# Second product: the high and low halves of B side by side, two matmuls in place of three

## The chip, the cores and the metric

One core of a Trainium2 chip runs the kernel. The metric is the device time of one execution in microseconds, as the median of several runs. The engines are TensorE (PE; its weight loads are listed as PEld), VectorE (DVE), ScalarE (ACT), GpSimd (POOL) and SyncE (SP), which issues most of the DMAs.

## The reference

Attention with a compressive memory for 4 batches x 8 heads x 576 positions x 64 dimensions, and behind it an expert layer over the 2304 rows that come out:

```
local = softmax(causal(q k^T / 8)) v
mem   = phi(q) M_prev / (phi(q) z_prev + 1e-6)        # phi(x) = elu(x) + 1
x     = (g * mem + (1 - g) * local) as [2304, 512]    # g = sigmoid(beta)
h     = x @ w_in                                      # [2304, 2048], the first product
r     = max(h, 0)
out   = (s * r * r + b) @ w_out                       # [2304, 512], the second product
```

## The kernel before

Precision comes from splitting. An fp32 operand x is kept as H = x rounded to fp32r and L = x - H, and a product of two such operands is H·H + H·L + L·H, three matmuls into one sum in PSUM.

The attention and the larger part of the first product are dealt out by a planner (class Plan). The rest of the first product is a hand-ordered list MM: L545 counts out what is left of batch 2, then for each of 16 column blocks f the 256 left-over rows (b = B, matmuls of 256 columns) and batch 3 (matmuls of 512 columns), each in two halves. t_mm1 issues one half, tick() moves a clock on by one, and later(n, ...) puts other work n ticks ahead. The outputs go through ScalarE's ReLU (L509) into r_d in DRAM.

Beside these ticks w_out is read as pairs of 32-bit words (load_u), converted (conv_u, conv64) and split. The second product is a Winograd form of a 2 x 2 block product: K is halved into KF = 8 blocks of 128, N into NE = 256 columns, rows into 128. It takes 7 products (numbered 1 to 7) for each of 9 tiles of 256 rows. split_u writes the high and low parts of five B operands into bHs and bLs, two tiles for each f. The B operands of products 4 and 2 (LATE) wait as fp32 in late32; late_b writes their high part into the room of w_in (slot w0H, free when half of the last ticks are done) and, in the first tile of the second product, their low part into w1H, which comes free with the last matmul of the first product.

For each tile, g_load reads r back into SRC, g_make squares, scales and shifts it (ScalarE), operand(t, m, c) makes the sums of A blocks and their H and L (two chunks c of four f each, eight buffers in all), product(t, m) issues 24 matmuls of 256 columns, and combine adds the results from PSUM into Y and U and stores them. SEQ is the order of the products; operands are issued AH = 2 products ahead, and g_make of the next tile from product 1 on. The source of even tiles lies in slot w0L, of odd tiles in w1L. The instructions of an engine run in order, and where the program does not pin it that order comes from the scheduler of the framework.

The lines that the change touches first of all are L714 to L716, the three matmuls, and L724 to L737, the additions.

Of the kernel before, what the change touches and what calls it, by code (L numbers as in the profile page):

```python
# [149 lines left out]
def attention_moe_kernel(  # L150
# [439 lines left out]
    PL = {m: n for n, m in enumerate((1, 3, 5, 6, 7))}  # L590
    w2 = ctx.enter_context(tc.tile_pool(name="w2", bufs=1, side="right", reuse_waits="tile"))
    bHs, bLs = {}, {}
    RAW = [0, 1, 2, 3, 4, 5, 6, 7, 4, 5, 6, 7, 8, 6, 7, 8]
    NRAW = 4
    NEXT = {n: (n + 4,) for n in range(9)} | {3: (), 4: (7, 8)} | {10: (13,), 11: (14,), 12: (15,)}

    def load_u(n):

        t = w2.tile([128, DM, 2], U32, tag=f"row{RAW[n]}", name="raw")
        r = n // 2 + n % 2 * KF  # L600
        nc.sync.dma_start(t, words(w_out)[128 * r:128 * r + 128])
        st["u", n] = t

    def stage(i):

        if i == 0:
            return stg0
        if i < 4:
            k = 4 + 2 * ((i + 1) % 2)
            return [w2.tile([128, 4, NE], F32, tag=f"bl{k + j}", name="stg1") for j in range(2)]  # L610
# [16 lines left out]
    def t_u(i, w, s):  # L627
# [6 lines left out]
        nc.vector.tensor_sub(late32[:, i, 0], t2, b21)  # L634

    def split_u(i, w, s):
        pin(nc.scalar.copy(late32[:, i, 1], w[:, 2]))
        bHs[i] = w2.tile([128, 5, NE], F32R, tag=f"row{i}", name="bH")
        bLs[i] = w2.tile([128, 5, NE], F32R, tag=f"bl{i}", name="bL")
        for x, a, n in ((w[:, 0:1], 0, 1), (w[:, 3:4], 1, 1), (s[:, 0:3], 2, 3)):  # L640
            L, H = bLs[i][:, a:a + n], bHs[i][:, a:a + n]
            pin(nc.scalar.copy(H, x))
            nc.vector.tensor_sub(L, x, H.bitcast(F32))

    def late_b(n, part):

        hs = slice(KF // 4 * n, KF // 4 * n + KF // 4)
        if part == 0:
            nc.scalar.copy(late[0][:, hs], late32[:, hs])
        else:  # L650
            nc.vector.tensor_sub(late[1][:, hs], late32[:, hs], late[0][:, hs].bitcast(F32))

    def b_op(m, f):
        if m in LATE:
            return [t[:, f, LATE.index(m)] for t in late]
        return bHs[f][:, PL[m]], bLs[f][:, PL[m]]

# [3 lines left out]
    def g_load(t):  # L661
        for f in range(0, NF, 4):
            c = 256 * (t % 2)
            nc.sync.dma_start(SRC[t % 2][:, f:f + 4], r_d[t // 2][:, f:f + 4, c:c + 256])
# [10 lines left out]
    def g_make(t, n):  # L675

        r = SRC[t % 2][:, NF // 4 * n:NF // 4 * n + NF // 4]
# [6 lines left out]
    def operand(t, m, c):  # L684

        r = SRC[t % 2]
        f1 = slice(4 * c, 4 * c + 4)
        f2 = slice(KF + 4 * c, KF + 4 * c + 4)
        A = {11: r[:, f1, 0:128], 12: r[:, f2, 0:128], 21: r[:, f1, 128:256], 22: r[:, f2, 128:256]}
        if m == 7 and not SUM:  # L690
# [5 lines left out]
        x = A[{1: 11, 7: 11, 5: 21, 6: 11, 3: 12, 2: 12, 4: 22}[m]]  # L696
# [11 lines left out]
    def product(t, m):  # L708
        ps = ps_y.tile([128, NE], F32, tag="y", name="yps")
        for f in range(KF):  # L710
            o = OPS[t, m, f // 4]
            H, L = o[:, 0, f % 4], o[:, 1, f % 4]
            BH, BL = b_op(m, f)
            nc.tensor.matmul(ps, lhsT=H, rhs=BH, start=f == 0, stop=False)  # L714
            nc.tensor.matmul(ps, lhsT=H, rhs=BL, start=False, stop=False)  # L715
            nc.tensor.matmul(ps, lhsT=L, rhs=BH, start=False, stop=f == KF - 1)  # L716
        OPS["ps", t, m] = ps

    def combine(t, m):
        ps = {n: OPS.get(("ps", t, n)) for n in SEQ}  # L720
        Y, U = YU[t % 2]
        add, sub = nc.vector.tensor_add, nc.vector.tensor_sub
        if m == 1:
            nc.scalar.copy(U[0], ps[1])  # L724
        elif m == 6:
            add(U[1], U[0], ps[6])
            add(U[2], U[1], ps[7])
            add(U[1], U[1], ps[5])
            add(Y[:, 1, NE:], U[2], ps[5])
            put_out(t, 1, slice(NE, DM), Y[:, 1, NE:])  # L730
        elif m == 3:
# [18 lines left out]
    stg0 = [w2.tile([128, 4, NE], F32, tag=f"row{i}", name="stg0") for i in (8, 7)]  # L750
    for i in range(4, 7):
        w2.tile([128, 5, NE], F32, tag=f"row{i}", name="row")
    late32 = w2.tile([128, KF, 2, NE], F32, tag="late", name="late32")
    for i in range(KF):
        w2.tile([128, 5, NE], F32, tag=f"bl{i}", name="blr")

    def slot16(tag, dtype):
        return wpool.tile([128, KF, 2, NE], dtype, tag=tag, name=tag)
# [94 lines left out]
```

## Time and profile before

| | us |
|---|---|
| median of 3 runs | 563.23 (560.71 to 563.55) |
| the profiled execution, its own time | 563.7 |
| its span | 561.6 |

Times in the profile's views are microseconds from the start of the span, unless marked ns. "Busy" of TensorE counts pipelined matmuls, so the length of one matmul is more than the distance to the next start. Where a view names what ended an engine's idle time, it stands in brackets with an arrow.

### The profile page before, as it was taken

What the parts mean: (1) busy time and instruction counts of PE and PEld (TensorE: products, weight loads), DVE (VectorE), ACT (ScalarE), POOL (GpSimd) and SP (SyncE); (2) the same over time, 40 slices, a digit from 0 to 9 for tenths busy, and PEclk for the clock granted to TensorE, in tenths of its full rate; (3) what the DMA queues carried; (4) which work ended last, traced back from release to release, by engine and by line L of the source; (5) the groups of instructions that cost most, each with busy time, mean ns of one, the idle gap of its engine ahead of it and who ended that gap; (6) DMA issues with size and microseconds to landing.
All of it is one profiled execution on the core that took longest, in us unless ns stands there. A gap on an engine that the chain in (4) does not pass through costs nothing.

```text
span 561.6 us, 11890 instructions
## 1 busy us (share of the span) xinstructions
PE 540.5 (96%) x4309; PEld 458.6 (82%) x4309; DVE 357.9 (64%) x884; ACT 399.4 (71%) x869; POOL 304.4 (54%) x327
## 2 busy tenths in 40 slices
PE   7978798999999999999999999999999999999997
PEld 5666576877777777777778888889999999999997
DVE  3888999999665264133309879137856786687562
ACT  5888977857867677246635657959779778877940
POOL 2587989577956646214310000324687678768850
PEclk9988999999999999999999999999999999999999
DMA  6643576684444441222147566447444435353101
GB/s 177 195 133 115 161 224 193 201 271 128 149 128 134 148 134 62 94 102 81 39 144 273 203 212 227 142 163 251 131 143 144 148 104 169 105 166 107 38 29 39
DMA packets 56666, 81.52 MB, mean 145 GB/s; under 512 B 7584, under 2 KB 39072, under 8 KB 56608
## 3 DMA queue, kind: packets, MB, share of 16 engines
q1 hardware_dynamic: 54592, 78.93, 44.2%
q10 hardware_dynamic: 2016, 1.84, 0.9%
q8 instruction: 34, 0.56, 0.4%
q14 instruction: 24, 0.20, 0.1%
HBM read 57.15 MB, written 23.59 MB: 144 GB/s over the span
## 4 chain that ended last, share of the span: by engine, by line
PE 87%; ACT 4%; DVE 4%; POOL 2%; issue 1%; POOLq 0%; ACTq 0%; DVEq 0%
PE yps L714 11%; PE yps L715 11%; PE yps L716 11%; PE sb L328 8%; PE tb L502 8%; PE tb L503 7%; PE tb L504 7%; PE sb L442 6%; PE hps L502 5%; PE hps L503 5%; PE hps L504 5%; PE tb L399 4%; ACT P L341 2%; DVE P L335 2%; POOL P L347 1%
## 5 line engine op out<-in xcount | busy, mean ns | idle before, releaser
L347 POOL TENSOR_SCALAR P<-P,sr,omg 128x192 f32<-128x192 f32 (+4 forms) x160 | 113.1, 724 | 58.0 <-DVE sr L375 37.4
L341 ACT ACTIVATE P<-P,mn 128x64 f32<-128x64 f32 (+4 forms) x160 | 88.6, 560 | 19.9 <-DVE mn L335 19.6
L714 PE MATMUL yps<-bH,op 128*128 128x256 f32 x360 | 101.2, 281 | 0.0
L715 PE MATMUL yps<-bL,op 128*128 128x256 f32 x360 | 101.1, 281 | 0.0
L716 PE MATMUL yps<-bH,op 128*128 128x256 f32 x360 | 101.1, 281 | 0.0
L335 DVE CUSTOM_DVE_ANT_0 P<-sb,mask 128x64 f32<-128x64 f32 (+4 forms) x160 | 69.8, 483 | 39.9 <-PE sb L328 39.8
L700 POOL TENSOR_TENSOR sum<-w0L 128x512 f32<-128x512 f32 x20 | 30.3, 1517 | 97.4 <-ACT w0L L680 75.8
L715 PEld LDWEIGHTS yps<-bL,op 128*128 128x128 f32 x360 | 67.9, 189 | 0.0
L716 PEld LDWEIGHTS yps<-bH,op 128*128 128x128 f32 x360 | 67.9, 189 | 0.0
L714 PEld LDWEIGHTS yps<-bH,op 128*128 128x128 f32 x360 | 67.8, 188 | 0.0
L328 PE MATMUL sb<-qk 64*128 64x288 f32 (+4 forms) x384 | 63.0, 450 | 2.7 <-DVE mn L335 2.7
L399 PEld LDWEIGHTS tb<-ident,P 64*128 64x128 f32 x928 | 40.3, 144 | 22.0 <-issue 5.5
L328 PEld LDWEIGHTS sb<-qk 64*128 64x128 f32 x384 | 41.1, 208 | 18.0 <-issue 8.0
L399 PE MATMUL tb<-ident,P 64*128 64x64 f32 x928 | 45.8, 234 | 10.0 <-POOL P L292 3.6
L523 ACT ACTIVATE r<-tb 128x512 f32<-128x512 f32 x41 | 24.4, 595 | 32.3 <-PE tb L504 26.4
L706 POOL TENSOR_TENSOR op<-w0L,op 128x512 fp32r<-128x512 f32 x30 | 42.4, 1433 | 6.3 <-ACT op L705 6.0
L409 ACT COPY pt<-tb 128x512 f32<-128x512 f32 x64 | 34.4, 589 | 11.0 <-PE tb L399 10.7
L700 POOL TENSOR_TENSOR sum<-w1L 128x512 f32<-128x512 f32 x16 | 24.5, 1531 | 31.9 <-DVE op L706 27.8
L705 ACT CAST op<-w0L 128x512 fp32r<-128x512 f32 x50 | 29.8, 615 | 16.1 <-PE yps L716 9.1
L502 PE MATMUL tb<-xs,w0H 128*128 128x512 f32 x96 | 40.4, 420 | 0.8 <-ACT pt L409 0.3
L714 PE MATMUL yps<-w0H,op 128*128 128x256 f32 x144 | 40.7, 283 | 0.0
L715 PE MATMUL yps<-w1H,op 128*128 128x256 f32 x144 | 40.7, 283 | 0.0
(136 smaller groups left out, 1439.7 us busy)
## 6 DMA issues: line engine op xcount, KB each, us to landing
r_d<-r SPq DMA_DIRECT2D x41, 256.0 KB, 2.1
w0L<-r_d SPq DMA_DIRECT2D x20, 512.0 KB, 4.7
qk<-in_qk_t_dram SPq DMA_DIRECT2D x15, 576.0 KB, 4.3
raw<-in_moe_w_out_dram SPq DMA_DIRECT2D x16, 512.0 KB, 5.3
w1L<-r_d SPq DMA_DIRECT2D x16, 512.0 KB, 4.5
xa<-in_moe_w_in_dram SPq DMA_DIRECT2D x12, 512.0 KB, 5.2
r_d<-r SPq DMA_DIRECT2D x48, 128.0 KB, 1.8
qs<-in_q_rows_dram SPq DMA_DIRECT2D x16, 320.0 KB, 4.0
```

Source lines behind the costliest of these rows:

```text
L328: nc.tensor.matmul(SB[ps[j]][:, o:o + n], lhsT=qk[rs, 128 * i:128 * i + 128], rhs=qk[rs, S + 64 + c0:S + 64 + c0 + n], start=True, stop=Tr ...
L335: nc.vector.tensor_tensor_reduce(P[:, j, PB[i] + 64:PB[i] + 64 + n], SB[ps[j]][:, o:o + n], m, -SCALE, 3.0e38, ALU.add, ALU.min, mn[:, j, ...
L341: nc.scalar.activation(pt, pt, AF.Exp, scale=-1.0, bias=mn[:, j, i:i + 1], accum_out=sm[:, j, i, 0:1])
L347: nc.gpsimd.tensor_scalar(pt, pt, sr[:, j, i:i + 1], omg[:, h:h + 1], ALU.mult, ALU.mult)
L399: nc.tensor.transpose(TB[ps[h]][:, o[h]:o[h] + 64], P[rs, j, c:c + 128], ident[rs, rs], tile_position=(64 * h, 0))
L502: nc.tensor.matmul(ps, lhsT=wH[:, p, fs], rhs=xs[:, 0], start=p == 0, stop=False)
L503: nc.tensor.matmul(ps, lhsT=wH[:, p, fs], rhs=xs[:, 1], start=False, stop=False)
L504: nc.tensor.matmul(ps, lhsT=wL[:, p, fs], rhs=xs[:, 0], start=False, stop=p == NP - 1)
L700: nc.gpsimd.tensor_sub(x, y, A[{7: 21, 3: 11}[m]])
L714: nc.tensor.matmul(ps, lhsT=H, rhs=BH, start=f == 0, stop=False)
L715: nc.tensor.matmul(ps, lhsT=H, rhs=BL, start=False, stop=False)
L716: nc.tensor.matmul(ps, lhsT=L, rhs=BH, start=False, stop=f == KF - 1)
```

## The change

B's high and low parts come to lie side by side in one tile (RB[i], shape [128, 5, 2, 256]; the late ones in two tiles of [128, 4, 2, 2, 256]). A step f of a product is then one matmul of H with 512 columns (BH and BL) and one of L with BH, 256 columns, onto the first half of the sum. The PSUM tile of a product is twice as wide, and combine adds both halves. SEQ is 1, 5, 6, 7, 3, 2, 4. The sign of late32's first part is turned, so product 4 is added. Both late parts are made as soon as the first slots w0H and w0L are free; the first tile's source takes the room of the fp32 late operands, the odd tiles' source takes w1H, and one of the output buffers w1L. The raw rows of w_out and their staging are dealt anew over the rooms of the B operands.

```diff
-    SEQ = [1, 7, 5, 6, 3, 2, 4]
+    SEQ = [1, 5, 6, 7, 3, 2, 4]
...
-        nc.vector.tensor_sub(late32[:, i, 0], t2, b21)
+        nc.vector.tensor_sub(T32[i // 2][:, i % 2, 0], b21, t2)
...
-        bHs[i] = w2.tile([128, 5, NE], F32R, tag=f"row{i}", name="bH")
-        bLs[i] = w2.tile([128, 5, NE], F32R, tag=f"bl{i}", name="bL")
+        RB[i] = w2.tile([128, 5, 2, NE], F32R, tag=f"rb{i}", name="rb")
...
-    def late_b(n, part):
-
-        hs = slice(KF // 4 * n, KF // 4 * n + KF // 4)
-        if part == 0:
-            nc.scalar.copy(late[0][:, hs], late32[:, hs])
-        else:
-            nc.vector.tensor_sub(late[1][:, hs], late32[:, hs], late[0][:, hs].bitcast(F32))
+    def late_b(n):
+
+        t = late[n // 2][:, 2 * (n % 2):2 * (n % 2) + 2]
+        H, L = t[:, :, :, 0], t[:, :, :, 1]
+        nc.scalar.copy(H, T32[n])
+        nc.vector.tensor_sub(L, T32[n], H.bitcast(F32))
...
-        if m in (7, 3):
-            y = x
-            x = SUM[c]
-            nc.gpsimd.tensor_sub(x, y, A[{7: 21, 3: 11}[m]])
-        elif m == 5:
-            nc.vector.tensor_add(x, x, A[22])
+        x = {1: a11, 5: SUM[c], 6: SUM[c], 2: a12, 7: a21, 3: SUM[c], 4: a22}[m]
+        if m == 5:
+            nc.vector.tensor_add(x, a21, a22)
         elif m == 6:
-            nc.vector.tensor_sub(x, A[21], x)
+            nc.vector.tensor_sub(x, x, a11)
+        elif m == 7:
+            nc.gpsimd.tensor_sub(x, a11, x)
+        elif m == 3:
+            nc.gpsimd.tensor_sub(x, a12, x)
...
-        ps = ps_y.tile([128, NE], F32, tag="y", name="yps")
+        ps = OPS["ps"] = ps_y.tile([128, 2, NE], F32, tag="y", name="yps")
         for f in range(KF):
             o = OPS[t, m, f // 4]
             H, L = o[:, 0, f % 4], o[:, 1, f % 4]
-            BH, BL = b_op(m, f)
-            nc.tensor.matmul(ps, lhsT=H, rhs=BH, start=f == 0, stop=False)
-            nc.tensor.matmul(ps, lhsT=H, rhs=BL, start=False, stop=False)
-            nc.tensor.matmul(ps, lhsT=L, rhs=BH, start=False, stop=f == KF - 1)
+            B = b_op(m, f)
+            nc.tensor.matmul(ps, lhsT=H, rhs=B, start=f == 0, stop=False)
+            nc.tensor.matmul(ps[:, 0], lhsT=L, rhs=B[:, 0], start=False, stop=f == KF - 1)
...
+        def onto(y, x):
+            add(y, x, ps[:, 0])
+            add(y, y, ps[:, 1])
+
+        if m in (1, 5):
+            u = U[0 if m == 1 else 3]
+            nc.scalar.copy(u, ps[:, 1])
+            add(u, u, ps[:, 0])
         elif m == 6:
-            add(U[1], U[0], ps[6])
-            add(U[2], U[1], ps[7])
-            add(U[1], U[1], ps[5])
-            add(Y[:, 1, NE:], U[2], ps[5])
+            onto(U[1], U[0])
+        elif m == 7:
+            onto(U[2], U[1])
+            add(U[1], U[1], U[3])
+            add(Y[:, 1, NE:], U[2], U[3])
             put_out(t, 1, slice(NE, DM), Y[:, 1, NE:])
         elif m == 3:
-            add(Y[:, 0, NE:], U[1], ps[3])
+            onto(Y[:, 0, NE:], U[1])
...
-            later(0, g_load, 0)
+            late.extend(slot16(f"w0{n}", F32R, [4, 2, 2, NE]) for n in "HL")
             for i in range(4):
-                later(LT + i, g_make, 0, i)
+                later(max(i, begin + CT[4 * i + 3] + 5 - clock[0]), late_b, i)
+            later(LT, first_load)
             for i in range(4):
-                later(max(LT + 4 + i, begin + CT[4 * i + 3] + 5 - clock[0]), late_b, i, 0)
+                later(LT + 6 + 2 * i, g_make, 0, i)
             for i in range(4):
-                later(LT + 8 + i, operand, 0, SEQ[i // 2], i % 2)
+                later(LT + 15 + i, operand, 0, SEQ[i // 2], i % 2)
...
-            if t == 0 and i < 4:
-                late_b(i, 1)
```

## Rows read from the trace of the kernel before

**Rows 1.** The page: busy us, share of the span, instructions of each engine.
```profile
PE 540.5 (96%) x4309; PEld 458.6 (82%) x4309; DVE 357.9 (64%) x884; ACT 399.4 (71%) x869; POOL 304.4 (54%) x327
```

**Rows 2.** Windows: length, busy PE, PEld, DVE, ACT, POOL, clock, DMA, GB/s.
```profile
292.00:378.00 86.00, 86.00 (x469) 74.85 (x470) 55.79 (x112) 58.04 (x126) 8.47 (x6) 1.00 0.62 207
378.00:558.00 180.00, 179.64 (x1513) 179.44 (x1511) 119.52 (x169) 136.50 (x198) 121.67 (x84) 1.00 0.39 124
438.00:458.00 20.00, 20.00 (x171) 20.00 (x170) 14.48 (x21) 16.16 (x24) 15.21 (x11) 1.00 0.44 134
```

**Rows 3.** By source line: count, duration ns min/median/max, first and last start.
```profile
L714 PE MATMUL yps<-bH,op x360: 277/281/285, 378.0 to 551.4; 128*128 128x256 f32 x180
...
L716 PE MATMUL yps<-w0H,op x144: 278/283/283, 392.4 to 557.4; 128*128 128x256 f32 x144
```

**Rows 4.** Timeline of TensorE, end of the first product: start, length, instruction.
```profile
365.42 0.28 PE L502 MATMUL hps<-x,w1H 128*128 128x256 f32 x1
365.53 0.28 PE L503 MATMUL hps<-x,w1H 128*128 128x256 f32 x1
...
366.85 0.40 PE L502 MATMUL hps<-xs,w1H 128*128 128x512 f32 x1
367.08 0.40 PE L503 MATMUL hps<-xs,w1H 128*128 128x512 f32 x1
367.32 0.39 PE L504 MATMUL hps<-xs,w1L 128*128 128x512 f32 x1
...
369.60 0.28 PE L502 MATMUL hps<-x,w1H 128*128 128x256 f32 x1
```

**Rows 5.** Groups, 378 to 558: busy, mean ns, idle before.
```profile
L706 DVE TENSOR_TENSOR op<-sum,op 128x512 fp32r<-128x512 f32 x34 | 23.3, 718 | 0.6 <-ACT op L705 0.6
...
L704 DVE TENSOR_TENSOR w0L<-w0L 128x512 f32<-128x512 f32 x8 | 13.2, 1653 | 0.9 <-POOL op L706 0.9
...
L702 DVE TENSOR_TENSOR w0L<-w0L 128x512 f32<-128x512 f32 x8 | 8.9, 1108 | 4.3 <-ACT w0L L680 4.3
...
L726 DVE TENSOR_TENSOR yu<-yu,yps 128x256 f32<-128x256 f32 x9 | 3.8, 421 | 42.0 <-PE yps L716 42.0
...
L724 ACT COPY yu<-yps 128x256 f32<-128x256 f32 x9 | 3.2, 352 | 0.7 <-PE yps L716 0.7
```

**Rows 6.** Timeline of the end, TensorE's last matmul and VectorE's last addition.
```profile
557.36 0.28 PE L716 MATMUL yps<-w0H,op 128*128 128x256 f32 x1
557.68 0.42 DVE L737 TENSOR_TENSOR yu<-yu,yps 128x256 f32<-128x256 f32 x1 [2.45 <-PE yps L716]
```

**Rows 7.** Waits from 378 to 558 (us, times, longest), then timeline in one tile.
```profile
ACT op L705 <- PE yps L716: 14.5, 19, 1.3
...
449.37 0.42 DVE L726 TENSOR_TENSOR yu<-yu,yps 128x256 f32<-128x256 f32 x1 [4.05 <-PE yps L716]
449.82 0.42 DVE L727 TENSOR_TENSOR yu<-yu,yps 128x256 f32<-128x256 f32 x1
...
452.71 3.46 POOL L706 TENSOR_TENSOR op<-w0L,op 128x512 fp32r<-128x512 f32 x2
```

**Rows 8.** Late operand and first tile: timeline, then the group of one line.
```profile
346.82 2.07 SPq L664 DMA_DIRECT2D w0L<-r_d  x4
...
353.03 1.04 ACT L649 CAST w0H<-late 128x1024 fp32r<-128x1024 f32 x1
...
349.46 1.29 DVE L643 TENSOR_TENSOR bL<-stg,bH 128x256 fp32r<-128x256 f32 x2
362.17 0.69 DVE L702 TENSOR_TENSOR w0L<-w0L 128x512 f32<-128x512 f32 x1 [11.42 <-issue]
...
362.94 3.00 POOL L706 TENSOR_TENSOR op<-w0L,op 128x512 fp32r<-128x512 f32 x2 [1.92 <-ACT op L705]
...
L651 DVE TENSOR_TENSOR w1H<-late,w0H x4: 1218/1220/1221, 379.9 to 383.3; 128x1024 fp32r<-128x1024 f32 x4
```

More of the change, by code (lines that the diff above doesn't have):

```diff
@@ L590, in attention_moe_kernel, with room @@
     PL = {m: n for n, m in enumerate((1, 3, 5, 6, 7))}
+    STG = {0: 7, 1: 6, 2: 5, 3: 7}
+    NEXT = {n: (n + 4,) for n in range(6)} | {7: (10, 11)} | {n: (n + 4,) for n in range(8, 12)}
     w2 = ctx.enter_context(tc.tile_pool(name="w2", bufs=1, side="right", reuse_waits="tile"))
[L592 to L595, printed above, removed]
+    RB = {}
+    T32 = [w2.tile([128, 2, 2, NE], F32, tag=f"late{i}", name="late32") for i in range(KF // 2)]
+    def room(k, dtype, name):
+        t = w2.tile([128, 2, 1280], dtype, tag=f"rb{k}", name=name)
+        return [t[:, h, :1024] for h in range(2)]
     def load_u(n):
-        t = w2.tile([128, DM, 2], U32, tag=f"row{RAW[n]}", name="raw")
+        if n % 2 == 0:
+            st["raw"] = room(n // 2, U32, "raw")
+        t = st["raw"][n % 2].rearrange("p (c b) -> p c b", b=2)
         r = n // 2 + n % 2 * KF
@@ L604, in stage @@
     def stage(i):
[L606 to L610, printed above, removed]
+        if i in STG:
+            return [t.rearrange("p (a e) -> p a e", e=NE) for t in room(STG[i], F32, "stg")]
         return stg[2 * (i % 2)], stg[2 * (i % 2) + 1]
@@ L661, in g_load @@
     def g_load(t):
-        for f in range(0, NF, 4):
+        for n in range(4):
             c = 256 * (t % 2)
-            nc.sync.dma_start(SRC[t % 2][:, f:f + 4], r_d[t // 2][:, f:f + 4, c:c + 256])
+            nc.sync.dma_start(SRC[t % 2][n], r_d[t // 2][:, 4 * n:4 * n + 4, c:c + 256])
     def put_out(t, h, cs, y):
@@ L675, in g_make @@
     def g_make(t, n):
[L677 removed]
+        r = SRC[t % 2][n]
         order = pin if t else same
@@ L686, in operand @@
         r = SRC[t % 2]
[L687 to L690, printed above, removed]
+        a11, a12, a21, a22 = r[c][:, :, 0:128], r[2 + c][:, :, 0:128], r[c][:, :, 128:256], r[2 + c][:, :, 128:256]
+        if not SUM:
             both = w2.tile([128, 2, 4, 128], F32, tag="row8", name="sum")
@@ L746, in attention_moe_kernel, with first_load, slot16 @@
     SUM = []
-    LT = 2
-    for i in range(NRAW):
-        load_u(i)
[L750 to L758, printed above, removed]
+    LT = 5
+    def first_load():
+        SRC.append([w2.tile([128, 4, 256], F32, tag=f"late{i}", name="src0") for i in range(4)])
+        g_load(0)
+    for i in range(4):
+        load_u(i)
+    for i in range(2, KF):
+        w2.tile([128, 2, 1280], F32, tag=f"rb{i}", name="rb")
+    def slot16(tag, dtype, shape):
+        return wpool.tile([128, *shape], dtype, tag=tag, name=tag)
     begin = clock[0]
@@ L778, in attention_moe_kernel @@
     flush()
-    late.append(slot16("w1H", F32R))
-    SRC.append(slot16("w1L", F32).rearrange("p f a (b n) -> p (f a b) n", n=256))
+    both = slot16("w1H", F32, [4, 4, 256])
+    SRC.append([both[:, n] for n in range(4)])
     YU = []
-    for t in (x4pool.tile([128, 2048], F32, tag="x4", name="yu0"), w2.tile([128, 2048], F32, tag="late", name="yu1")):
+    for t in (x4pool.tile([128, 2048], F32, tag="x4", name="yu0"), wpool.tile([128, 2048], F32, tag="w1L", name="yu1")):
         YU.append((t[:, :1024].rearrange("p (j e) -> p j e", j=2),
-                   [t[:, 1024 + NE * k:1024 + NE * k + NE] for k in range(3)]))
+                   [t[:, 1024 + NE * k:1024 + NE * k + NE] for k in range(4)]))
     p3.close()
```

27 lines of the change are left out of this document (10 added, 17 removed).

## The prediction

> **What bounds the kernel now.** I read the page first, for the busy shares: TensorE is busy for 96% of the span, no other engine for more than 71% [rows 1]. An average over stages says little about one stage, so next come the windows by stage. The change touches two of them. From 292 to 378 us (the end of the first product) TensorE is busy for all of 86.00 us, and from 378 to 558 (the second product) for 179.64 of 180.00, at a granted clock of 1.00, the level of 2.4 GHz, in both [rows 2]. Nothing stalls TensorE in the second product, so what it costs is the spacing of its matmuls. The by-line view gives that spacing: the first matmul starts at 378.0, the last at 557.4, and there are 9 tiles x 7 products x 8 x 3 = 1512 of them, so (557.4 - 378.0) / 1511 = 0.1187 us each [rows 3]. The listed 0.28 us of one matmul is its pipelined length and no part of a sum. The other engines follow from the window of one tile of 20 us: VectorE 14.48 busy, ScalarE 16.16, GpSimd 15.21 [rows 2]. They are beside the path, but not by much, and this decides how much of a gain can be kept.
>
> **Matmuls: three become two.** For each of 8 x 63 = 504 steps, H x BH and H x BL (256 columns each) become one matmul of 512 columns, and L x BH stays. The columns are the same 768; what goes is one matmul with its weight load. Before, a step costs 3 x 0.1187 = 0.3562 us. The kernel already runs matmuls of 512 and 256 columns next to each other at the end of the first product [rows 4], and two prices come out of that stretch. (a) At the seams: 512 after 256 takes 367.08 - 366.85 = 0.23, 256 after 512 takes 365.53 - 365.42 = 0.11, a step of 0.34. (b) A whole round of twelve 256s and twelve 512s: 369.60 - 365.42 = 4.18, divided by 12 is 0.348. In the new order every matmul stands at a seam, so (a) is the nearest row, but it is a difference of two times printed to 0.01 (0.32 to 0.36 with rounding), while (b) is averaged. I take 0.346, between them and nearer to the averaged one. That saves 0.3562 - 0.346 = 0.0102 us a step, 504 x 0.0102 = 5.1 us. The bounds: 0.348 saves 4.1 us; 0.34 saves 8.2 us.
>
> The rows thus show a fixed part in every matmul: two 256s cost 2 x 0.1187 = 0.237 us, one 512 some 0.227 to 0.229 (0.346 or 0.348 less 0.1187), so 8 to 10 ns go with the instruction and not with its columns. The Trainium skill (TensorE: Matmul & The Clock Gate, section "Wait — 56ns, not 53.3ns?") puts the fixed part of a warm matmul at about 2.5 ns. By that page the change would save 504 x 2.5 ns = 1.3 us, an estimate from the page alone. The trace does not agree, with 8 to 10 ns [rows 3, 4].
>
> **Combining: one sum in PSUM becomes two.** H x BL now collects in columns of its own, so each product needs one addition more. Per tile VectorE goes from 7 additions that read PSUM to 14, at 0.42 us each [rows 5]: 2.9 us more of VectorE, and one copy of 0.35 us more of ScalarE. They lie beside the matmuls, except the last one: after the final matmul starts at 557.36, the addition at 557.68 and the output DMA are the path to the end [rows 6]. The second of two dependent additions starts 0.45 us after the first (449.37 and 449.82, where one uses the other's result) [rows 7]. The tail grows by 0.45 us.
>
> Beside the matmuls the cover is as follows. A tile's 168 matmuls at 0.1187 are 19.94 us now, and its 56 steps at 0.346 will be 19.38. VectorE then needs 14.48 + 2.9 = 17.4 of 19.38 us, ScalarE 16.2 + 0.4 = 16.5, GpSimd its same 15.2. So all fit, VectorE with 2.0 us to spare where it had 5.5. What can spoil that is order. VectorE runs in order, and today it waits for TensorE at almost one place in a tile alone: the first addition of product 6, 42.0 us for 9 of them, 4.7 us a tile [rows 5]. After the change every product ends with additions, seven such places, and those of products 1 and 5 wait for a ScalarE copy too. Behind a waiting addition stand the sums and low parts of the next operands, and TensorE waits for these. Against that stands the lead: ScalarE waits 19 times for TensorE to free an operand buffer [rows 7], so operands are as far ahead as the eight buffers let them, and GpSimd starts on the low parts of a tile's first operand at 452.71 [rows 7], while that product starts only at about 458 (product 6 ends at 449.4 by the addition it releases, and three more of 2.85 us follow). The work takes 3.46 us, which leaves about 2 us of slack. The PSUM pool has eight buffers, one for each product, so a late addition alone stops nothing. I cost this edit at nothing, and its bound is in the rivals.
>
> SEQ changes too (1, 5, 6, 7 for 1, 7, 5, 6), with the same number of sums per tile; product 5 is now second, so its sum a21 + a22 is due one product earlier. These sums are the slow ones: 1.65 and 1.11 us on average, for a size that the low part of a sum takes 0.72 for [rows 5]. No fewer of them are made, so I see no gain here; the cost is zero or the stall of rival 1.
>
> **The late operands and the first tile's source.** Before, the high part of the late operand is made in the first product and its low part in the second, four subtractions of 1.22 us at 379.9 to 383.3 [rows 8]. These move up into VectorE's empty time between 350.8 and 362.2 [rows 8]: nothing, and 4.9 us less for VectorE in the first tile. But their room pushes the first tile's source out: it now takes the place of late32, so the load has to wait for the late operand, where before it was issued at 346.82 [rows 8]. From that load to the end of GpSimd's low parts of product 1's operand (362.94 + 3.00 = 365.9) it was 19.1 us, ReLUs of the stores, squares, scales and casts included. The last quarter of the new load can be issued when ScalarE's last late copy (353.03 + 1.04) and its subtraction (1.22) are done, at 355.3, so the operand is there at 355.3 + 19.1 = 374.4. It is due at 378.0 [rows 3], product 5's operand 2.8 us later. That leaves 3.6 us. On SyncE the stores of r stand behind the waiting load; held up for some us, they hold ScalarE's ReLUs, and these the pool of eight PSUM tiles, each of which takes TensorE 2.1 us on average (4.18 us for two, [rows 4]), so 16 us of cover. I cost it at nothing; the bound is 2.8 us, if the 19.1 us become a third more.
>
> The raw weights, stage buffers and their places are re-dealt, with the same 16 loads, conversions and splits. Their end at 350.8 [rows 8] starts the chain above, and a shift by 3 us stays within its slack. The first four loads may wait a little longer or shorter for room; nothing but this chain hangs on them.
>
> **The sum.** The profiled execution took 563.7 us by its own time (span 561.6, 2.1 around it). 563.7 - 5.1 + 0.45 = 559.05. It lies 0.5 us above the median of 563.23, so against the median I say 558.6.
>
> **The rivals.**
> 1. Operand stalls eat half of the gain or all of it. With 2.0 us of VectorE to spare a tile, TensorE would stop for 0.3 to 0.6 us a tile, where a sum for product 5 or 6 meets GpSimd's work behind a waiting addition: 9 x 0.3 to 0.6 = 2.7 to 5.4 us, so 561.3 to 564.0. For it: 17.4 of 19.38 us. Against: the lead, and no stall today. 18%.
> 2. VectorE becomes the bound, the case on the other side. Its place is the seven ordered waits of a tile, its price the part of them that exceeds 2.0 us. Today's waits are 4.7 us a tile in one place. If 3.2 us of them stay, a tile takes 17.4 + 3.2 = 20.6, 1.2 us over 19.38, and 9 tiles give 11 us: 569.6; with 3.8 it is 575. It is slower than before from 2.5 us of waits a tile on (0.5 over, times 9, is the whole gain). Against: a wait shrinks when its engine runs late. 10%.
> 3. The start of the second product is missed: the chain above lands past 378 by 2 to 3 us, 560.6 to 561.6. 6%.
> 4. The fixed part goes with the columns and not with the instruction, so the change doesn't do what it says: a 512 costs 2 x 0.1187 = 0.237 and the step 0.356, no gain, and the tail on top gives 563.7. The slowest 512 comes near (367.08 to 367.32 is 0.24 [rows 4]). 5%. The Trainium skill's page, with its 2.5 ns, would come close to this time: 563.7 - 1.3 + 0.45 = 562.9, or 562.4 against the median.
> 5. Steps at 0.34: 555.5. 8%.
>
> **Chances.** The forecast has 53%. A measurement of this kernel can tell about 0.5%, so 560.4 is the border. Faster, the forecast and rival 5 with the mildest end of rival 3: 0.62. Same, rivals 1, 3 and 4 for the most part: 0.26. Slower, rival 2 and a bad end of rival 1: 0.12. The range from 555.5 to 563.8 leaves out rival 2, the worst of rival 1 and a little below, some 16%.
>
> **What would show it.** In the profile after, the steady step should be 0.340 to 0.349 with the 512s near 0.23 and 256s near 0.11; the second product should last 504 x 0.346 = 174.4 us in place of 179.6, with no gap longer than a step. The window of a tile should have VectorE near 17.4, and the first product should still be full from 292 on and end at 378.0. Gaps before the first matmul of a product, above all of 5 and 6, released by VectorE, would be rivals 1 and 2; a gap at 378 rival 3; a 512 at 0.237 rival 4. The prediction is wrong in its core if the step is outside 0.340 to 0.349 or if TensorE is less than 99% busy after 378.

## The result

The changed kernel takes 567.86 us (median of 4 runs, 567.84 to 570.09) against 562.88 for the kernel before on the same chip: a ratio of 1.0105, 95% interval 1.0068 to 1.0142. It is about 1% slower, where 558.6 us, and so faster, was forecast. The profiled execution of after took 567.84 us by its own time (span 565.7), 4.1 us more than the one of before (563.7).

The page of after, engines (busy us, share, instructions), and the first line of its chain, beside [rows 1]:

```profile
PE 539.5 (95%) x3805; PEld 431.8 (76%) x3805; DVE 407.4 (72%) x947; ACT 400.0 (71%) x878; POOL 305.6 (54%) x327
...
PE 61%; DVE 16%; ACT 14%; issue 4%; POOL 4%; ACTq 0%; POOLq 0%; DVEq 0%
```

504 matmuls are gone (4309 to 3805), TensorE's share falls, and 30% of the chain runs through VectorE and ScalarE, where the page of before has 8%. The windows of after, columns as in [rows 2]:

```profile
292.00:378.00 86.00, 86.00 (x472) 74.93 (x471) 61.84 (x118) 59.26 (x130) 7.40 (x6) 1.00 0.59 206
...
400.00:550.00 150.00, 145.44 (x812) 123.61 (x812) 134.99 (x188) 117.64 (x174) 103.87 (x72) 1.00 0.35 111
...
438.00:458.00 20.00, 19.44 (x110) 16.47 (x109) 17.63 (x28) 16.33 (x24) 14.07 (x11) 1.00 0.43 131
```

The first product is as full as before. In the second, TensorE is idle for 4.56 us of 150, where it was idle for 0.36 of 180 [rows 2]. In the window of 20 us VectorE and ScalarE sit where the prediction put them, at 17.6 and 16.3. The granted clock is 1.00 as before.

From its first matmul to its last the second product takes 376.55 to 560.96 = 184.41 us, 5.0 more than before (179.4, [rows 3]). Its nine tiles, from the first matmul of one to that of the next (the ninth: to its own last), take 19.52, 19.70, 20.51, 20.73, 20.27, 20.91, 20.79, 20.98 and 21.0 us; before, each took 19.95. So the first two tiles gain and the others lose.

**Who keeps TensorE waiting.** The waits of after from 376 to 562 (us, times, longest):

```profile
ACT op L704 <- DVE sum L699: 26.6, 14, 3.4
...
PEld yps L714 <- DVE op L705: 9.2, 15, 1.5
```

TensorE waits for low parts (L705), and ScalarE, which casts the high parts (L704), waits for VectorE's sum for product 6 (L699). The wait that [rows 7] showed before, ScalarE for `PE yps` (19 times, a buffer not yet free), is down to two in this window. ScalarE's timeline shows why (start, length, instruction, idle before and releaser; it is busy without a gap in the lines left out):

```profile
441.14 1.23 ACT L704 CAST op<-sum 128x512 fp32r<-128x512 f32 x2 [3.41 <-DVE sum L699]
...
455.33 1.24 ACT L681 ACTIVATE src<-src,b_sb,s_sb 128x1024 f32<-128x1024 f32 x1
456.48 0.60 ACT L704 CAST op<-sum 128x512 fp32r<-128x512 f32 x1
457.60 0.62 ACT L704 CAST op<-sum 128x512 fp32r<-128x512 f32 x1 [0.52 <-DVE sum L697]
461.62 0.62 ACT L704 CAST op<-sum 128x512 fp32r<-128x512 f32 x1 [3.41 <-DVE sum L699]
```

VectorE and GpSimd at the same place:

```profile
454.95 0.84 DVE L697 TENSOR_TENSOR sum<-src,src 128x512 f32<-128x512 f32 x1 [1.34 <-ACT src L681]
...
456.60 0.91 DVE L697 TENSOR_TENSOR sum<-src,src 128x512 f32<-128x512 f32 x1 [0.48 <-ACT src L681]
...
457.76 3.15 DVE L705 TENSOR_TENSOR op<-sum,op 128x512 fp32r<-128x512 f32 x2
460.83 0.68 DVE L699 TENSOR_TENSOR sum<-sum,src 128x512 f32<-128x512 f32 x1
```
```profile
456.91 3.46 POOL L701 TENSOR_TENSOR src<-src 128x512 f32<-128x512 f32 x2
```

This is a loop that closes over one tile. VectorE's sum for product 5 (L697) waits for ScalarE's last shift of the tile's source (L681). ScalarE's next casts wait for that sum and for the one of product 6 (L699), which on VectorE stands behind the low parts of product 5. And behind these casts, in ScalarE's order, stand the squares and shifts of the next tile (L680, L681), for which the next sums will wait. TensorE is not part of it. One turn, from one cast to the same a tile later, takes 461.62 - 441.14 = 20.48 us: ScalarE's work of the tile and 3.9 us of waits at the seam. The four turns from 441.14 on, up to 524.30, take 20.8 us on average.

**It was there before.** ScalarE's casts of product 6 in the trace of before, and in the last line a cast that waits for a free buffer:

```profile
440.35 0.62 ACT L705 CAST op<-w1L 128x512 fp32r<-128x512 f32 x1 [2.29 <-DVE w1L L704]
...
456.81 0.62 ACT L705 CAST op<-w0L 128x512 fp32r<-128x512 f32 x1 [0.99 <-DVE w0L L704]
459.71 0.62 ACT L705 CAST op<-w0L 128x512 fp32r<-128x512 f32 x1 [2.28 <-DVE w0L L704]
...
495.01 0.62 ACT L705 CAST op<-w0L 128x512 fp32r<-128x512 f32 x1 [0.86 <-PE yps L716]
```

One turn took 459.71 - 440.35 = 19.36 us, and TensorE's tile 19.95, so the loop hid with 0.59 us to spare. The turns around it are as long: the same cast starts at 421.00, 440.35, 459.71, 479.06 and 498.43. The new loop, in the turn shown, is 1.1 us longer (0.35 of it the second copy, 0.7 longer waits, 3.93 for 3.27), against a TensorE tile that is only 0.27 us shorter (19.68, in e5 and e7 below).

### The profile page after: what moved, and what is told of

Read it like the earlier page. It is cut to its first block, busy times and chain, and to the rows that moved or that the text cites. A ratio compares the mean times of both kernels' runs of the same rounds, so it can differ in the third digit from the quotient of the medians.

```text
span 565.7 us, 10940 instructions
## 1 busy us (share of the span) xinstructions
PE 539.5 (95%) x3805; PEld 431.8 (76%) x3805; DVE 407.4 (72%) x947; ACT 400.0 (71%) x878; POOL 305.6 (54%) x327
## 4 chain that ended last, share of the span: by engine, by line
PE 61%; DVE 16%; ACT 14%; issue 4%; POOL 4%; ACTq 0%; POOLq 0%; DVEq 0%
PE sb L328 8%; PE tb L502 8%; PE tb L503 6%; PE tb L504 6%; PE sb L442 6%; DVE op L705 6%; PE hps L502 5%; PE hps L503 5%; PE hps L504 5%; PE tb L399 4%; PE yps L713 4%; ACT op L704 4%; POOL P L347 2%; DVE sum L697 2%; PE yps L714 2%
## 5 line engine op out<-in xcount | busy, mean ns | idle before, releaser
L713 PE MATMUL yps<-rb,op 128*128 128x512 f32 x360 | 126.6, 394 | 0.0
L714 PE MATMUL yps<-rb,op 128*128 128x256 f32 x360 | 101.8, 285 | 4.6 <-DVE op L705 4.4
L705 POOL TENSOR_TENSOR op<-src,op 128x512 fp32r<-128x512 f32 x30 | 41.8, 1412 | 90.1 <-ACT op L704 86.2
L713 PEld LDWEIGHTS yps<-rb,op 128*128 128x128 f32 x360 | 67.3, 188 | 14.8
L714 PEld LDWEIGHTS yps<-rb,op 128*128 128x128 f32 x360 | 67.8, 188 | 9.4 <-DVE op L705 9.2
L704 ACT CAST op<-sum 128x512 fp32r<-128x512 f32 x54 | 33.4, 620 | 38.6 <-DVE sum L699 26.6
L705 DVE TENSOR_TENSOR op<-sum,op 128x512 fp32r<-128x512 f32 x54 | 53.9, 1014 | 8.0 <-ACT op L704 7.9
L502 PE MATMUL tb<-xs,w0H 128*128 128x512 f32 x96 | 40.3, 420 | 0.8 <-ACT pt L409 0.3
L292 POOL TENSOR_TENSOR P<-qs,nrm 128x384 f32<-128x384 f32 (+1 forms) x30 | 23.5, 802 | 31.0 <-PE tb L399 15.4
L705 POOL TENSOR_TENSOR op<-w1H,op 128x512 fp32r<-128x512 f32 x24 | 32.9, 1395 | 12.3 <-PE yps L714 5.5
L503 PE MATMUL tb<-xs,w0H 128*128 128x512 f32 x96 | 37.7, 392 | 0.0
L504 PE MATMUL tb<-xs,w0L 128*128 128x512 f32 x96 | 37.5, 390 | 0.0
L509 ACT ACTIVATE r<-hps 128x256 f32<-128x256 f32 x62 | 21.3, 384 | 16.2 <-DMA r_d<-r 11.8
```

The costliest lines, as they stand in the source:

```text
L502: nc.tensor.matmul(ps, lhsT=wH[:, p, fs], rhs=xs[:, 0], start=p == 0, stop=False)
L503: nc.tensor.matmul(ps, lhsT=wH[:, p, fs], rhs=xs[:, 1], start=False, stop=False)
L504: nc.tensor.matmul(ps, lhsT=wL[:, p, fs], rhs=xs[:, 0], start=False, stop=p == NP - 1)
L705: (nc.gpsimd if m in ONPOOL else nc.vector).tensor_sub(L, x, H.bitcast(F32))
L713: nc.tensor.matmul(ps, lhsT=H, rhs=B, start=f == 0, stop=False)
L714: nc.tensor.matmul(ps[:, 0], lhsT=L, rhs=B[:, 0], start=False, stop=f == KF - 1)
```

## The experiments

Four theories stand in the expectations. A, in its first form, puts the loop down to the room that the sums of products 5 and 6 share; A2 is the loop through ScalarE's order as above. B: VectorE has too much to do (seven more additions a tile). P: the new places of the operands, or the late operands, cost the time. "Steady tile" is the distance between first matmuls of neighbouring tiles, for the sixth to the eighth tile of the profiled execution; the second product runs from its first matmul's start to its last one's. In e1, e2 and so on the edit is to the kernel after unless another is named.

| | median us | ratio to before, 95% interval | second product us | steady tile us |
|---|---|---|---|---|
| after | 567.86 | 1.0105, 1.0068 to 1.0142 | 184.4 | 20.8 to 21.0 |
| e1 own room for sum 6 | 566.76 | 1.0059, 1.0039 to 1.0080 | 184.1 | 20.5 to 20.6 |
| e2 old order | 566.35 | 1.0053, 1.0031 to 1.0075 | 182.4 | 20.83 |
| e3 no second additions | 568.04 | 1.0086, 1.0057 to 1.0116 | 184.8 | 20.9 to 21.1 |
| e4 three matmuls | 568.27 | 1.0085, 1.0059 to 1.0111 | 185.4 | 21.05 |
| e5 no shift pass | 560.70 | 0.9949, 0.9932 to 0.9966 | 176.9 | 19.68 |
| e6 old order, three matmuls | 562.11 | 0.9984, 0.9967 to 1.0002 | 179.4 | 19.95 |
| e7 old order, no second additions | 559.62 | 0.9938, 0.9909 to 0.9966 | 176.9 | 19.68 |
| e8 e1 without second additions | 567.22 | 1.0073, 1.0045 to 1.0101 | 183.8 | 20.5 to 20.7 |
| e9 before, casts doubled | 570.28 | 1.0138, 1.0100 to 1.0176 | 187.8 | 20.9 to 21.4 |
| e10 shift folded | 582.30 | 1.0329, 1.0293 to 1.0366 | 189.5 | 21.2 to 22.4 |
| e11 old order, folded | 567.69 | 1.0081, 1.0054 to 1.0108 | 176.3 | 19.53 |
| e12 e11, root moved | 569.41 | 1.0107, 1.0073 to 1.0141 | 176.3 | 19.53 to 19.56 |
| e13 e11, root held late | 559.98 | 0.9968, 0.9950 to 0.9985 | 176.3 | 19.53 to 19.56 |

**e1: own room for the sum of product 6.**

```diff
-        x = {1: a11, 5: SUM[c], 6: SUM[c], ..., 3: SUM[c], 4: a22}[m]
+        x = {1: a11, 5: SUM[c], 6: SUM6 and SUM6[c], ..., 3: SUM6 and SUM6[c], 4: a22}[m]
...
-            nc.vector.tensor_sub(x, x, a11)
+            nc.vector.tensor_sub(x, SUM[c], a11)
```

> The changed kernel, but the sum for product 6 goes into a buffer of its own (in unused room beside one output buffer), where the change overwrites product 5's sum with it and so must wait for product 5's low part. Nothing else is altered; VectorE's work is the same. Theory A (a closed loop per tile: ScalarE stands in its queue at the cast of product 6's operand until VectorE has done sum 5, low part 5 twice and sum 6; the squares and scales of the next tile stand behind it, and the next sum 5 needs them; 15.9 us of ScalarE and about 4.6 of VectorE make the 20.5 us a tile seen after the change): the 3.1 us of low part 5 leave the loop, the tile falls to TensorE's 19.4 and the run to 558.5 to 560.5. Theory B (VectorE has too much work, 18 us of additions, sums and low parts a tile): no change, 566 to 568.

The room was not the cause, and theory A in its first form falls. The time is in B's range, and this kernel can't rule B out: VectorE is busy for 144.0 us from 400 to 550, 9 more than in after. ScalarE's waits change place (for product 5's sum 1.96 us, for product 6's 2.27), and one turn is still 462.06 - 441.47 = 20.59 us:

```profile
441.47 0.62 ACT L704 CAST op<-yu 128x512 fp32r<-128x512 f32 x1 [2.26 <-DVE yu L699]
458.65 0.62 ACT L704 CAST op<-sum 128x512 fp32r<-128x512 f32 x1 [1.96 <-DVE sum L697]
462.06 0.62 ACT L704 CAST op<-yu 128x512 fp32r<-128x512 f32 x1 [2.27 <-DVE yu L699]
```

**e2: the old order of products, with wide matmuls and second additions.**

```diff
-    SEQ = [1, 5, 6, 7, 3, 2, 4]
+    SEQ = [1, 7, 5, 6, 3, 2, 4]
...
-            onto(U[2], U[1])
-            add(U[1], U[1], U[3])
-            add(Y[:, 1, NE:], U[2], U[3])
+            onto(U[2], U[1], OPS["ps", t, 7])
+            onto(U[1], U[1], OPS["ps", t, 5])
+            onto(Y[:, 1, NE:], U[2], OPS["ps", t, 5])
```

> The changed kernel with the old order of the products (1, 7, 5, 6, 3, 2, 4) and the old places of their sums (5 and 6 in place over the source, where sum 6 need not wait for low part 5); the two wide matmuls, the second additions and the early late operand stay. VectorE makes 15 additions from PSUM a tile in place of 14, of which two had both operands in SBUF. Theory A: the loop is open, TensorE sets the tile, 559 to 561. Theory B: VectorE's work falls by about 1 us a tile at most, 563 to 567.

The old order alone doesn't bring the gain back, and again the time lies in B's range. ScalarE's two waits for the sums of product 6 are 1.81 and 2.96 us here, where the kernel before has 0.99 and 2.28. That is 1.5 us more, and 19.36 + 1.5 = 20.86 is close to the tile of 20.83. Three additions from PSUM now stand between these two sums on VectorE, where before there were none; e7, which differs in the second additions alone, shows that they are the cause. How they act is argued: the first sum (L699 at 496.52) is also held for 1.20 us by GpSimd's low part of product 1 (L705), which by the program still reads the room that the sum overwrites.

```profile
498.37 0.62 ACT L704 CAST op<-src 128x512 fp32r<-128x512 f32 x1 [1.81 <-DVE src L699]
501.95 0.62 ACT L704 CAST op<-src 128x512 fp32r<-128x512 f32 x1 [2.96 <-DVE src L699]
```

**e3: no second additions.** H·BL is left out of the sum for five of the seven products.

```diff
-            add(y, y, ps[:, 1])
```

> The changed kernel without the second addition of products 6, 7, 3, 2 and 4, so that H x BL of these five is left out of the output; TensorE's work is the same. VectorE loses five additions of 0.42 us a tile. Theory A: only what stands between sum 5 and cast 6 shortens the loop, one or two additions, 0.4 to 0.8 us a tile: 561 to 564.5. Theory B: VectorE falls from 18 to 16 us a tile and all of the stall goes: 557.5 to 559.5.

The time lies outside both forecasts. VectorE is relieved of 13 us in 150 (134.99 in after), some 1.8 us a tile, and the tile is as long as ever. That speaks against B.

```profile
400.00:550.00 150.00, 143.91 (x810) 123.43 (x809) 121.72 (x153) 117.13 (x172) 100.93 (x71) 1.00 0.35 111
```

**e4: three matmuls of 256 columns into one sum, all else as after.**

```diff
-            nc.tensor.matmul(ps, lhsT=H, rhs=B, start=f == 0, stop=False)
+            nc.tensor.matmul(ps[:, 0], lhsT=H, rhs=B[:, 0], start=f == 0, stop=False)
+            nc.tensor.matmul(ps[:, 0], lhsT=H, rhs=B[:, 1], start=False, stop=False)
...
-            add(y, y, ps[:, 1])
...
-            nc.scalar.copy(u, ps[:, 1])
-            add(u, u, ps[:, 0])
+            nc.scalar.copy(u, ps[:, 0])
```

> The changed kernel with the matmuls of before (three of 256 columns a step, one sum in PSUM) and so without the second additions; order of the products, places of the sums, late operands and layout stay as changed. This is the order of the products alone. Theory A: the loop without the additions in it takes 19.7 to 20.1 us against TensorE's 19.94, so 562.5 to 565. Theory B: as before the change, 562 to 563.5.

Neither the wide matmul nor a second addition is in this kernel, and it loses as much as after does, outside both forecasts again. VectorE has 15.29 us of work in 20, ScalarE waits at the seam again, and a turn is 504.57 - 483.51 = 21.06 us. The window first, then ScalarE:

```profile
480.00:500.00 20.00, 19.43 (x161) 19.03 (x161) 15.29 (x20) 16.40 (x24) 13.16 (x10) 1.00 0.38 117
```
```profile
483.51 0.62 ACT L704 CAST op<-sum 128x512 fp32r<-128x512 f32 x1 [2.80 <-DVE sum L699]
...
501.15 0.62 ACT L704 CAST op<-sum 128x512 fp32r<-128x512 f32 x1 [1.10 <-DVE sum L697]
504.57 0.62 ACT L704 CAST op<-sum 128x512 fp32r<-128x512 f32 x1 [2.80 <-DVE sum L699]
```

**e5: ScalarE's second pass over the source (scale and shift) left out.**

```diff
-        order(nc.scalar.activation(r, r, AF.Identity, scale=s_sb, bias=b_sb))
```

> The changed kernel without ScalarE's second pass over the source (times s, plus b), which is left out of the output; everything else is as changed, VectorE's and GpSimd's work too. Theory A2 (a closed loop through ScalarE's queue: it stands at the casts of products 5 and 6 until VectorE has made their sums, the next tile's squares and shifts stand behind, and the next sums need those; its length is ScalarE's work of some 16 us and 4 to 5 us of waiting, 20.6 to 21 us a tile in every variant so far): 4.6 us of ScalarE's work leave the loop, 16.3 is far below TensorE's 19.4, so 558 to 560. Theory B (VectorE's work, or its contention with GpSimd): no change, 566 to 568.

All of the change is in this kernel, the new order and all additions, and TensorE runs without a gap (150.00 of 150); ScalarE waits for free buffers again (L703 is the cast here, L698 the sum for product 6):

```profile
400.00:550.00 150.00, 150.00 (x855) 130.82 (x854) 136.75 (x199) 89.46 (x150) 116.63 (x76) 1.00 0.36 113
```
```profile
ACT op L703 <- DVE sum L698: 45.6, 14, 4.4
ACT op L703 <- PE yps L713: 7.2, 14, 0.8
```

VectorE does more than in after, 136.75 us, since the tiles come faster. So B falls, and the loop through ScalarE is shown to be the limit: four passes less in a turn, 456.48 - 455.33 = 1.15 us each from start to start, take 4.6 us out of it and bring it below TensorE's tile.

**e6 and e7: the two causes apart, both in the old order of e2.** e6 has e4's three matmuls and single sum; e7 has the wide matmul and leaves out the second additions (H·BL is missing in all products but product 1).

> Old order of the products and three matmuls a step with one sum in PSUM: what is left of the change is the early late operand, the new places of source, raw weights and buffers. Theory A2: neither the order nor the additions lengthen the loop, it falls to the 19.4 us that it had before, below TensorE's 19.94, so 562 to 564. Theory P (the new places make the slower tile, since both the order and the additions have been taken out alone without effect): 566 to 568.

> Wide matmuls in the old order without the second addition (H x BL of all products but product 1 is left out of the output). Theory A2: the loop has nothing in it that the kernel before had not, 19.4 us, as long as TensorE's wide tile of 19.5: 558 to 560. Theory P: 566 to 568. Theory B: 558 to 560 as well.

Both run without gaps. e6 equals before in time, with the new places and late operands: P falls, and so does any cost of the first product. With e4 (new order, no additions: 21.05), e6 (neither: 19.95), e2 (old order, additions: 20.83) and e7 (neither: 19.68), either the new order or the second additions lengthens the loop past TensorE, and both together (after) not by more than one. In the second product, the new order, with its places of the sums, costs 185.4 - 179.4 = 6.0 us (e4 against e6), the second additions 182.4 - 176.9 = 5.5 (e2 against e7), both 184.4 - 176.9 = 7.5 (after against e7).

**e8: e1 without second additions** (H·BL is left out as in e3).

> Wide matmuls, the new order with a buffer of its own for sum 6, and without the second additions (H x BL of five products left out of the output). Theory A2: the loop of the own buffer, 20.6 us, loses the additions that stand among the sums, 0.4 us each, two or three of them: 19.5 to 20, so 559 to 562.5. Theory P: 566 to 568.

A2 expected 559 to 562.5 here and was wrong: the tile hardly moves against e1. From 400 to 550 us ScalarE waits 13.5 us for the sum of product 5 and 13.0 us for GpSimd's sum of product 3, and no run tells why these stay so long. In the new order no single relief of VectorE opens the loop.

**e9: the loop of before made longer.** Two casts of the kernel before are done twice (products 2 and 4, 2.2 us a tile of ScalarE).

```diff
         nc.scalar.copy(H, x)
+        if m in (2, 4):
+            nc.scalar.copy(H, x)
```

> The kernel before the change, with the casts of products 2 and 4 done twice (the same values again), 4 x 0.51 = 2.05 us more for ScalarE a tile, which then works 18.3 of 19.95 us. Theory A2: the loop through ScalarE's queue was there before the change already, 19.4 us long and hidden under TensorE's 19.95; now it is 21.4, so once the lead of some 3 us is used up every tile loses 1.45 us: 570 to 575. If no such loop existed before: ScalarE still has 1.6 us to spare a tile, 562 to 564.

2.2 us on an engine that was busy for 16.2 of 20 cost 8.4 us in the second product. ScalarE has 17.37 us of work in 20, yet TensorE idles; a turn, here from a cast of product 5 (whose sum is L702) to the next tile's, is 502.79 - 481.86 = 20.93. So the loop was under TensorE before the change.

```profile
480.00:500.00 20.00, 19.26 (x163) 19.06 (x162) 13.37 (x20) 17.37 (x27) 12.87 (x10) 1.00 0.39 126
```
```profile
481.86 0.62 ACT L705 CAST op<-w1L 128x512 fp32r<-128x512 f32 x1 [0.63 <-DVE w1L L702]
...
502.79 0.62 ACT L705 CAST op<-w0L 128x512 fp32r<-128x512 f32 x1 [0.64 <-DVE w0L L702]
```

**e10 to e13: the whole computation, with a shorter ScalarE pass.** The square takes the root of s as its scale, and the shift b goes into the cast and the low part, so the pass of e5 isn't needed. The sums for 5 and 6 go to GpSimd, which keeps those for 7 and 3; VectorE makes all low parts but those of 7 and 3. e10 is in the new order, e11 to e13 in the old.

```diff
-        order(nc.scalar.activation(r, r, AF.Square))
-        order(nc.scalar.activation(r, r, AF.Identity, scale=s_sb, bias=b_sb))
+        order(nc.scalar.activation(r, r, AF.Square, scale=q_sb))
...
-        nc.scalar.copy(H, x)
-        (nc.gpsimd if m in ONPOOL else nc.vector).tensor_sub(L, x, H.bitcast(F32))
+        if m in (7, 3):
+            nc.scalar.copy(H, x)
+            nc.gpsimd.tensor_sub(L, x, H.bitcast(F32))
+        else:
+            bb = b2_sb if m == 5 else b_sb
+            nc.scalar.activation(H, x, AF.Identity, bias=bb)
+            nc.vector.scalar_tensor_tensor(L, x, bb, H.bitcast(F32), ALU.add, ALU.subtract)
```

> The changed kernel, complete in what it computes, with ScalarE's second pass folded away: s goes into the square as its root, b is added where the high and low parts are made (in ScalarE's cast as its bias, in VectorE's subtraction as its scalar). [...] Theory A2: ScalarE has 11.8 us a tile and the loop falls below TensorE's 19.7, 560 to 562. If VectorE or GpSimd (12 operations of 1.3 to 1.5 us, 17 us a tile) binds instead: 564 to 568.

> The same folding in the old order of the products (1, 7, 5, 6, 3, 2, 4), wide matmuls and second additions kept, complete in what it computes. Theory A2: 560 to 562, TensorE sets the tile. If VectorE or GpSimd binds: 564 to 568.

e10 is worse, by far more than either forecast: ScalarE's casts (L710) now wait for GpSimd's sums for product 6 (L700), which wait for VectorE's low parts (L711) in their turn (first fence, from 400 to 560). e11 has the short second product, but starts it at 383.35 us (before: 378.0). e12, where the root of s stands in the middle of the first product in the program, starts it at 387.52 and misses both of its forecasts for the whole time:

> The folded kernel in the old product order (e11_old_folded), with the one square root that it needs taken in the middle of the first product instead of at the start, so that ScalarE neither waits for s there (5.0 us in e11's rows) nor changes its table twice ahead of the softmax (two table loads of 1.28 us). Theory of the ScalarE loop: the second product stays as in e11, 176.3 us with a tile of 19.5 us and TensorE busy without gaps, and the stretch before it falls back to that of the kernel before, so the whole takes 559 to 561 us, ratio 0.993 to 0.997 against the kernel before. Rival (e11's longer start is due to something else, such as the places of the two new constants): the stretch before the second product stays some 6 us longer and the time stays at 566 to 568 us, ratio about 1.008.

The scheduler had moved the root and the doubling of b to the start in both. In e12 VectorE and ScalarE wait there for s and b, which come late in SyncE's queue, and the attention behind them waits (second fence):

```profile
ACT op L710 <- POOL sum L700: 48.1, 16, 5.6
POOL sum L700 <- DVE op L711: 25.4, 16, 3.3
```
```profile
19.24 0.15 DVE L779 TENSOR_SCALAR b_sb<-b_sb 128x1 f32<-128x1 f32 x1 [9.15 <-DMA b_sb<-in_moe_b_dram]
...
18.82 0.20 ACT L778 ACTIVATE q_sb<-s_sb 128x1 f32<-128x1 f32 x1 [5.68 <-DMA s_sb<-in_moe_s_dram]
```

In e13 both are pinned to their place:

```diff
+            pin(nc.scalar.activation(q_sb, s_sb, AF.Sqrt))
+            pin(nc.vector.tensor_scalar(b2_sb, b_sb, 2.0, None, ALU.mult))
```

> As e12_late_sqrt (shift folded away, old product order, 512-column matmuls, the complete computation), but with the square root and the doubling of b held at their place in the middle of the first product: in e12 both had been moved to the start of the kernel, where VectorE waited 9.2 us for b and ScalarE 5.7 us for s. Theory of the ScalarE loop: the second product stays at 176.3 us with tiles of 19.53 us, the start is that of the kernel before again, and the whole takes 558.5 to 561 us, ratio 0.992 to 0.997. Rival (something else in the folded kernel lengthens the stretch before the second product): that stretch stays 6 to 10 us longer, 566 to 570 us, ratio 1.006 to 1.012.

```profile
400.00:555.00 155.00, 151.82 (x869) 132.60 (x868) 150.20 (x196) 95.20 (x136) 133.66 (x86) 1.00 0.35 110
...
438.00:458.00 20.00, 20.00 (x117) 17.55 (x116) 19.86 (x26) 13.36 (x20) 18.61 (x13) 1.00 0.42 132
```

The start is that of before again, the whole takes 559.98 us against 561.92 (12 and 17 runs), and the second product is 3.1 us shorter than that of before (176.3 for 179.4), with nothing left out. VectorE, at 19.86 of 20 us, has nothing to spare in that window.

## Why the prediction was wrong

**The step that failed: two terms put at nothing.** Of the second additions the prediction says "I cost this edit at nothing", of the new order "the cost is zero or the stall of rival 1". For both it added up each engine's work in a tile, compared it with TensorE's 19.38 us and found it to fit. In the window of one tile the sums came close (VectorE 17.6, ScalarE 16.3, GpSimd 14.1); from 400 to 550 VectorE is at 18.0 of 20. But what sets the tile is a turn of a loop, work and waits of three engines in series, 20.5 to 21.1 us. It cost 184.41 - 176.86 = 7.5 us against the same matmuls without stalls (e7), and either term alone would have cost 5.5 to 6.0. Both signs that the prediction named for being wrong in its core came: a step of 0.351 us (e5, e7), and TensorE at 145.44 of 150, or 97%.

**The evidence used for the lead was misread.** The 19 waits of ScalarE for a free buffer [rows 7] were taken as a standing lead. By window, in the trace of before, three of them lie between 400 and 478 us, and all others later: the lead builds up by 0.6 us a tile. It was the sign of a loop that is nearly as long as TensorE's tile. The waits for L704 in the same view (13.3 us in eight, the longest 2.3) were not followed back.

**Rivals 1 and 2.** The outcome (567.9) lies between rival 1 (up to 564.0) and rival 2 (569.6 to 575), and rival 2's mechanism isn't the one: VectorE was not the bound (e3, e4 and e5 each show it), and of its seven ordered waits little appeared. Over the whole second product of after VectorE waits 2.4 us for PSUM at L722, and 5.0 us at L728 for ScalarE's copy. Rival 1's stalls were the right kind (PEld waits for L705), but priced at 2.7 to 5.4 us, and by VectorE's load.

**The matmul step was mis-sized.** The seam row gave 0.23 and 0.11 us; in after 512 columns take 0.23 or 0.24 us to the next start, 256 take 0.12. Seven steps of after, at a change from one operand's room to another:

```profile
450.33 0.39 PE L713 MATMUL yps<-rb,op 128*128 128x512 f32 x1
450.56 0.28 PE L714 MATMUL yps<-rb,op 128*128 128x256 f32 x1
...
451.37 0.40 PE L713 MATMUL yps<-w0H,op 128*128 128x512 f32 x1
...
452.78 0.40 PE L713 MATMUL yps<-w0L,op 128*128 128x512 f32 x1
```

The first three steps take 1.04 / 3 = 0.347 us, as forecast; the next four 1.41 / 4 = 0.353. Over a steady tile without stalls (e5, e7) the mean is 19.68 / 56 = 0.3514. So 504 steps save 179.4 - 176.86 = 2.55 us, half of the 5.1 forecast, 5.1 ns for each matmul removed. Taking the averaged row (0.348) would have been nearer, and still too low.

This mean hides two levels, which the matmuls of 256 columns have too. Each pair of lines runs from the first matmul of a product to the first one of product 2, over five products of eight steps in before, four in e13 and five in e5:

```profile
457.75 0.28 PE L714 MATMUL yps<-bH,op 128*128 128x256 f32 x1
471.95 0.28 PE L714 MATMUL yps<-w0H,op 128*128 128x256 f32 x1
```
```profile
456.46 0.39 PE L719 MATMUL yps<-rb,op 128*128 128x512 f32 x1
467.56 0.40 PE L719 MATMUL yps<-w0H,op 128*128 128x512 f32 x1
```
```profile
456.00 0.39 PE L712 MATMUL yps<-rb,op 128*128 128x512 f32 x1
470.12 0.40 PE L712 MATMUL yps<-w0H,op 128*128 128x512 f32 x1
```

Before, a step of these products takes 14.20 / 40 = 0.355 us (and 0.359 in products 2 and 4); in e13 11.10 / 32 = 0.347, which saves the 8 ns that the prediction read as the fixed part; in e5 14.12 / 40 = 0.353, which saves 2. So what failed was less the fixed part than the level, for which the prediction had no row. With e13's tile of 19.53 a removed matmul is worth 0.42 us / 56 = 7.5 ns. The Trainium skill (TensorE: Matmul & The Clock Gate, section "Wait — 56ns, not 53.3ns?") gives 2.5 ns for a warm matmul's fixed part; the measured 5.1 and 7.5 ns lie between it and the forecast's 10.

**The additions were under-priced.** All 14 were costed at the 0.42 us of additions that read PSUM. Two of them, L733 and L734, read only SBUF (from 400 to 550 us; columns: duration ns min/median/max, first and last start):

```profile
L722 DVE TENSOR_TENSOR yu<-yu,yps x36: 404/409/423, 399.9 to 545.2; 128x256 f32<-128x256 f32 x36
...
L733 DVE TENSOR_TENSOR yu<-yu x7: 568/1289/1401, 408.5 to 533.7; 128x256 f32<-128x256 f32 x7
L734 DVE TENSOR_TENSOR yu<-yu x7: 410/1516/1523, 409.0 to 534.9; 128x256 f32<-128x256 f32 x7
```

Alone L734 takes 0.41 us, but mostly 1.5: GpSimd works at the same time, and additions from PSUM never stretch (404 to 423 ns). Each stretched one of the two lines ends 0.28 to 0.29 us after the end of one of GpSimd's instructions, as at 452.82 after one that ended at 452.53. The low parts of product 5 likewise take 3.15 us for two beside GpSimd's L701 above, and 0.68 each when alone. The Trainium skill (SBUF — State Buffer, section "SBUF: two separate sides") says that VectorE, when both its inputs are in SBUF, and a GpSimd instruction that reads SBUF lock each other out for a whole instruction; these rows agree. The two long additions aren't needed for the loss, though: e2 has neither and is slow too.

**What was right.** The first product stayed full, and the late operands and the first tile's chain cost nothing: the second product begins at 376.55 without a gap (rival 3 is out). Rival 4 (no gain) is out, as the step is 0.351 us in the mean and not 0.356, though at the higher level a 512 comes close to two 256s. The tail is one addition longer, 561.73 - 561.27 = 0.46 us:

```profile
561.27 0.42 DVE L722 TENSOR_TENSOR yu<-yu,yps 128x256 f32<-128x256 f32 x1 [1.75 <-PE yps L714]
561.73 0.42 DVE L723 TENSOR_TENSOR yu<-yu,yps 128x256 f32<-128x256 f32 x1
```

**The sum again, as it should have been.** From 563.7: -2.55 for the matmuls, +7.5 for the loop, +0.45 for the tail, -1.4 for a second product that began earlier in this execution (376.55 for 378.0) gives 567.7; it took 567.84. The loop's term is the difference of two measured stretches, so this is an account and no second forecast. The earlier start is chance: in after and e1 to e8 the second product begins anywhere from 374.4 to 379.0 us.

**Still open.** Why a step has two levels (0.347 and 0.353 with the wide matmul, 0.355 and 0.360 before), which change by product and differ between kernels with the same matmuls (e13's tile of 19.53 has more of the low one than e5's 19.68), no run tells. Nor does any show why the loop stays long in e8, or how much of the longer seam in the new order is due to GpSimd's interference and how much to the sums of 5 and 6 standing next to each other.

## What to carry to other kernels

A kernel with one engine at 100% can have a second limit just under it that no busy share shows: a loop over tiles through the in-order queue of an engine that is 80% busy. Look for it by taking one instruction that waits and its twin a tile later: if the distance stays below the bound's tile by a few per cent only (19.36 to 19.95 us here), a gain on the bound is worth no more than that, and a wait added at the seam counts once the difference is used up. The sign of slack is the engine waiting for a free buffer in every tile; count such waits by tile, not over the stage.

## What the runs showed of the hardware

A matmul of 512 columns between two of 256 has no single price: about 0.230 us in some products and about 0.230 and 0.240 by turns in others (e5), at the same granted clock of 1.00 (the level of 2.4 GHz). VectorE's instructions with both inputs in SBUF went from 0.41 to 1.52 us and from 0.68 to 1.80 beside GpSimd's, those with an input in PSUM not at all. And two tiny instructions that wait for two loads of 0.5 KB, moved to the start of the kernel by the scheduler, cost 6 to 9 us of the whole (e11 and e12 against e13: 7.7 and 9.4 us by their medians, 6.4 and 7.8 by their ratios to before).
